# A new issue order for every engine of a clustered attention and feed-forward kernel

## The chip, the core and the metric

The kernel runs on one NeuronCore of a Trainium2 chip. The core has five engines with their own instruction queues, each of which runs in order: TensorE (PE; its weight loads are listed as PEld), VectorE (DVE), ScalarE (ACT), GpSimd (POOL) and SyncE (SP), which here only issues DMAs. The metric is the device time of one execution in microseconds, the median of several runs.

## The reference, cut to what matters

Attention of 4 batches x 8 heads x 768 tokens x 64 features, in which a query sees only the keys of its own cluster (the nearest of 16 centroids of its head), and then a feed-forward layer of 3072 tokens, 512 to 1024 to 512, with a softmax-weighted activation and a layer norm inside:

```python
q_assign = np.argmax(np.einsum('bhsd,hcd->bhsc', q_n, c_n), axis=-1)   # and k_assign
mask = q_assign[:, :, :, None] == k_assign[:, :, None, :]
scores = np.where(mask, scale * np.matmul(q, k.transpose(0, 1, 3, 2)), -1000000000.0)
attn = softmax(scores);  x = matmul(attn, v)        # heads side by side: 3072 x 512
h = x @ w_in
solu = h * softmax(h)
ln = (solu - mu) / np.sqrt(var + 1e-06) * g_ln
out = ln @ w_out
```

## The kernel before, in words

**Names.** The program is a list of about 1,800 small named operations. A name is a kind and an index; `ca1.0.1.1`, for example, is a cast for batch 1, head pair 0, k (1; q is 0), second head of the pair. The kinds, with their lines:

- SP: `ld` loads raw q or k of a head pair (L374 whole for batch 0, L402 in quarters of 96 KB after that), `lv` loads v (L518), `lo` and `li` load w_out and w_in (L555, L539), `tx` turns the attention output x into the feed-forward's left operand by a transposing DMA (L662), `tu` does the same for the activation u (L715), `ou` stores the output (L781).
- Attention operands: `tp` (PE, L386) with `xa` (copy out, L396), or `xt` (DVE, L410), turn raw q and k; `ca` casts them into the score operand `qk` (L434, L436, L438); `cv` casts v (L523). `cl` (PE, L448 and L453) scores the tokens against the centroids; `tb`, `mx`, `oh`, `ot` (DVE, L462, L475, L480, L486) turn that, take the maximum, make the one-hot rows and turn them back; `pl` places those rows below q and k in `qk` (L498 and L505 by an engine, L503 by a DMA), and `bl` blanks the rows of the other head (L514). The one-hot rows make the score of an own-cluster pair larger by a constant, which is how the mask gets into one matmul.
- Attention: `S` is one PSUM bank of scores (PE, L584), `E` its exponential (ACT, L590), `V` the product with v for 128 queries (PE, L607; a column of ones gives the denominator), `N` the division (DVE, L619 and L632) for a group of them.
- Feed-forward, 24 tiles of 128 tokens: `h` (PE, L693, four parts a tile), `hm` the row maximum (DVE, L699), `ex` the exponential (ACT, L705), `u` the product with h (DVE, L710), `bn` and `ag` the statistics (DVE, L721, L725), `at` and `al` the row's scale (POOL, L731, L737, L740), `y` (PE, L754, four parts a tile), `sc` the scaling (ACT L769 or DVE L771). The last tiles are turned on TensorE (`ptx`, `ptu`) and copied out by `tx` and `tu` operations of DVE or ACT (L674, L687, L689).
- Weights, once: `su` sums w_out times the gain (DVE, L559 and L562), `me` (PE) spreads the mean, `ce` centres w_out (DVE, L570), `wi` casts w_in (L542). `fl` are idle matmuls early on.

**Tiling.** Raw tiles have 8 buffers, turned ones 6, score operands 6 head pairs, score banks in PSUM 3, their exponentials 9. One PSUM bank collects `V` of a group until `N` has read it. Three banks take the halves of `h` of two tiles in turn.

**What sets the order.** `Weave.ORDER` holds, for every engine, a written-out list of kinds with counts (`ld4` is the next four `ld`), and `Weave.AWAY` says which operations run on another engine than the one they name by default. Within a kind and engine, operations come in the order in which they were added. `queues()` turns the lists into queues of names and asserts that every operation is used up; `run()` walks the queues with costs and due times, and issues the instructions in the order of the starts that it finds. Each engine's own order is therefore exactly its list. An instruction waits on its engine, with all that is behind it, until its operands and its buffer are there; the synchronisation is put in from the tiles that it reads and writes.

```python
for kind, n in re.findall(r"([A-Za-z]+)(\d*)", text):
    for _ in range(int(n or 1)):
        queues[e].append(of[e, kind].pop(0))
```

Of the kernel before, what the change touches and what calls it, by code (L numbers as in the profile page):

```python
# [22 lines left out]
class Weave:  # L23
# [19 lines left out]
    ORDER["PE"] = """
        wm tp2 cp tp cl tp fl5 cl tp2 S3 tp2 S2 cq S tp S tp S2 cl V3 S2 tp S gt tp S3 V3 cl S3 tp2
        S2 V2 S V S2 tp S2 tp S2 V3 S3 cl S V S2 V3 S3 cl S2 V S V2 S V S5 V2 S2 V2 S3 V S2 V2 S V
        S3 V3 S V S2 me S3 V3 S V S2 cl S2 V2 S2 V2 S h S h S2 h S h S2 V3 S V h S2 h V2 S V2 S2 h2
        S3 h2 S2 V4 S2 y3 V S y V S3 h2 S V2 S2 h2 V2 S cl S2 V2 h S2 h S h V S2 V3 S h S2 y3 S y V
        S2 V h y S3 y3 S h S2 V3 cl S2 V S V2 S y S2 y S V h S V y S h V S V y S3 V2 cl S2 h S V2 S2
        V S V2 S V S h S2 cl V4 S3 y2 S2 y S V S V2 S V S2 y S V2 S2 h2 S2 h V S2 V h S2 h V4 y2 S2
        y h y S2 V2 h S h S2 cl S V4 S2 h cl S3 h3 S2 V S V y S h S y V S y V3 S3 h y h S2 h V2 S2 y  # L50
        h2 S y S V2 S y V y V3 S3 h2 S2 cl h S2 h S cl S3 V4 y V y S3 y V y S3 h2 S V S V cl S V4 S2
        y S y S2 y V S y V S V S2 V y2 S y S2 V2 S V2 S2 y S V2 S2 V2 S h S2 h S h2 S2 V S h V y S y
        V3 h S y S2 y V S2 h2 V2 S V S V S cl S2 V h2 S y S V S2 h2 S3 y V S V2 h2 V2 S V S2 h2 S3
        h2 S V y S2 V2 y S V3 S h2 S h S2 V2 y V2 S y h y S3 h2 S2 V S y V3 S3 h2 y S V S h V2 h S3
# [19 lines left out]
    """
    AWAY = {}
    AWAY.update(dict.fromkeys("""
        ca0.0.0.0.1 ca0.1.1.0 ca0.2.0.0 ca0.2.1.1 ca1.3.0.0 ca2.2.0.0 ca2.3.1.0 sc23.0 tu22.1
        xa0.0.0.1 xa0.0.1.0 xa0.1.0.0 xa0.2.1.0 xa0.2.1.1
    """.split(), "ACT"))
    AWAY.update(dict.fromkeys("""  # L80
        bl1.2 ca0.1.0.1 ca1.3.0.1 ca2.1.0.1 ca3.2.0.1 ca3.3.0.0 cv0.1.0 cv1.0.1 cv1.1.1 cv2.0.0
        cv2.0.1 cv2.1.0 cv2.1.1 cv2.2.1 cv3.0.0 cv3.3.0 pl0.0.0.1.1 pl0.1.0.0 pl0.1.1.0 sc0 sc13
        sc14 sc19 sc20 sc22 sc23.1 sc9 tu22.0 wi3 xa0.0.0.0
    """.split(), "DVE"))
    AWAY.update(dict.fromkeys("""
        ca0.0.1.1.0 pl0.0.0.0.0 pl0.0.1.1.0 pl1.0.0.0 pl1.0.0.1 pl1.0.1.1 pl1.1.0.0 pl1.1.0.1
        pl1.1.1.0 pl1.1.1.1 pl1.2.0.0 pl1.2.0.1 pl1.2.1.0 pl1.2.1.1 pl1.3.0.0 pl1.3.0.1 pl1.3.1.0
        pl1.3.1.1 pl2.0.0.0 pl2.0.0.1 pl2.0.1.0 pl2.0.1.1 pl2.1.0.0 pl2.1.0.1 pl2.1.1.0 pl2.1.1.1
        pl2.2.0.0 pl2.2.0.1 pl2.2.1.1 pl2.3.0.0 pl2.3.0.1 pl2.3.1.1 pl3.0.0.0 pl3.0.0.1 pl3.1.0.1
        pl3.1.1.0 pl3.1.1.1 pl3.2.1.0 pl3.2.1.1 pl3.3.0.0  # L90
    """.split(), "POOL"))
    HOP = 0.17
    LANES = 8
# [1132 lines left out]
```

## Time and profile before

| | before |
|---|---|
| median of 3 runs | 228.74 us (228.43 to 230.03) |
| span of the profiled execution | 230.3 us |
| its own time beside the span | not given |
| PE busy | 218.3 us (95%) |
| DVE busy | 202.9 us (88%) |
| ACT busy | 195.9 us (85%) |
| POOL busy | 122.8 us (53%) |
| TensorE clock granted | 1.00 of full speed |
| moved by DMA | 39.15 MB, of which 115,128 of 125,472 packets are under 512 B |

The profile is of one execution; the span reaches from its first to its last instruction. Busy time is the union of an engine's instructions. Ends of matmuls are modelled, so a busy PE is not PE at its peak, and spans on POOL are rough. A group's row gives the line, engine, operation, tiles, shapes and count, then busy time, the mean of one in ns, and the idle time before them with what ended it. In the rows by stretch, each engine's busy time in the stretch comes in the order PE, PEld, DVE, ACT, POOL.

### The profile page before, as it was taken

The numbers are of one execution on the slowest core, as the hardware profiler recorded it, in microseconds if no ns is written. First come the engines' busy times: TensorE is split into PE (matmuls) and PEld (weight loads), VectorE is DVE, ScalarE is ACT, GpSimd is POOL, SyncE is SP. The second block draws the span as 40 slices with busy tenths as digits, with TensorE's granted clock in tenths as the row PEclk, the third lists the DMA queues.
The fourth block names the chain that finished last, engine by engine and source line by source line (L and its number), as shares of the span: only waits on it lengthen the run. The fifth ranks groups of instructions, "written<-read, shape, count | busy, mean of one in ns | idle before, by whom it ended". The sixth has DMA issues, their size and how long they took to land.

```text
span 230.3 us, 6600 instructions
## 1 busy us (share of the span) xinstructions
PE 218.3 (95%) x2393; PEld 149.0 (65%) x2424; DVE 202.9 (88%) x363; ACT 195.9 (85%) x379; POOL 122.8 (53%) x241
## 2 busy tenths in 40 slices
PE   6999898999999999899999899999999999999994
PEld 3566465767767777576667657786677777665352
DVE  3599999999999997999999879887998894987993
ACT  2689889999999999798999889999999998785350
POOL 4555789639663835593349969546915130233311
PEclk9999999999999999999999999999999999999999
DMA  6996989488799989999999999999245118668623
GB/s 147 358 311 151 245 174 324 161 162 150 151 195 175 158 221 170 131 250 160 201 149 204 183 163 197 222 170 238 56 100 128 47 25 124 152 94 178 177 78 117
DMA packets 125472, 39.15 MB, mean 170 GB/s; under 512 B 115128, under 2 KB 120192, under 8 KB 125440
## 3 DMA queue, kind: packets, MB, share of 16 engines
q1 hardware_dynamic: 123696, 38.21, 79.5%
q10 hardware_dynamic: 1744, 0.52, 0.9%
q8 instruction: 19, 0.31, 0.6%
q14 instruction: 13, 0.11, 0.2%
HBM read 23.11 MB, written 6.29 MB: 128 GB/s over the span
## 4 chain that ended last, share of the span: by engine, by line
PE 57%; DVE 19%; POOL 8%; DMA 6%; issue 4%; SPq 4%; ACT 1%; DVEq 0%; POOLq 0%; ACTq 0%
PE sps L584 16%; PE hreg L693 13%; PE yps L754 13%; PE ops L607 9%; PE csc L453 3%; DMA raw<-in_k_dram 3%; SPq L402 3%; DMA w_st<-in_moe_w_in_dram 3%; DVE xt L410 2%; DVE u L710 2%; POOL qk L505 2%; PE hreg L386 2%; POOL qk L436 2%; POOL qk L438 1%; DVE x L632 1%
## 5 line engine op out<-in xcount | busy, mean ns | idle before, releaser
L590 ACT ACTIVATE e<-sps 128x512 bf16<-128x512 f32 (+1 forms) x294 | 150.4, 605 | 11.0 <-PE sps L584 9.8
L584 PE MATMUL sps<-qk 96*128 96x256 bf16 (+5 forms) x636 | 95.5, 264 | 2.1 <-POOL qk L505 0.8
L584 PEld LDWEIGHTS <-qk 96*128 96x128 bf16 (+1 forms) x636 | 60.6, 121 | 30.6 <-issue 9.2
L607 PEld LDWEIGHTS <-e 128*128 128x128 bf16 x1152 | 50.2, 97 | 11.9 <-DVE x L632 1.6
L607 PE MATMUL ops<-v,e 128*128 128x65 bf16 x1152 | 54.7, 193 | 1.6 <-POOL v L523 0.9
L693 PE MATMUL hreg<-w_in_sb,xT 128*128 128x512 bf16 x176 | 49.1, 379 | 1.5 <-DVE u L710 0.6
L754 PE MATMUL yps<-w_out_c,uT 128*128 128x512 bf16 x169 | 46.9, 378 | 0.7
L705 ACT ACTIVATE e_sb<-hreg,nmax 128x1024 bf16<-128x1024 f32 x24 | 26.8, 1118 | 8.5 <-DVE nmax L699 8.3
L505 POOL COPY qk<-oht 32x384 f32<-32x384 f32 (+1 forms) x42 | 21.2, 504 | 22.8 <-DVE oht L486 16.1
L710 DVE TENSOR_TENSOR u<-e_sb,hreg 128x1024 bf16<-128x1024 bf16 x24 | 28.9, 1205 | 4.9 <-ACT e_sb L705 3.4
L721 DVE BATCH_NORM_STATS2 bs<-u 128x6 f32<-128x512 bf16 x48 | 31.5, 676 | 0.2
L699 DVE TENSOR_REDUCE nmax<-hreg 128x1 f32<-128x1024 f32 x24 | 28.9, 1206 | 2.3 <-PE hreg L693 2.2
L410 DVE STREAM_TRANSPOSE xt<-raw 128x768 f32<-128x768 f32 x24 | 23.1, 961 | 2.8 <-DMA raw<-in_k_dram 1.6
L754 PEld LDWEIGHTS <-uT 128*128 128x128 bf16 x200 | 17.9, 97 | 10.9 <-DVE uT L687 0.7
L438 POOL TENSOR_SCALAR qk<-xt 64x768 bf16<-64x768 f32 (+1 forms) x28 | 23.7, 848 | 1.6
L693 PEld LDWEIGHTS <-xT 128*128 128x128 bf16 x192 | 16.8, 97 | 11.0 <-DVE u L710 1.2
L737 POOL TENSOR_SCALAR esq<-es,mv 128x1 f32<-128x1 f32 x24 | 8.1, 339 | 27.8 <-DVE mv L725 22.7
L436 POOL CAST qk<-xt 64x768 bf16<-64x768 f32 (+1 forms) x25 | 20.4, 817 | 3.9 <-DVE xt L396 1.6
L731 POOL TENSOR_SCALAR es<-esum 128x1 f32<-128x1 f32 x24 | 5.9, 246 | 30.9 <-ACT e_sb L705 30.4
L632 DVE TENSOR_TENSOR x<-ops,den 128x256 bf16<-128x256 f32 (+1 forms) x39 | 18.9, 485 | 1.3
L740 POOL TENSOR_TENSOR alpha<-esq,halves 128x1 f32<-128x1 f32 x24 | 14.6, 606 | 2.0
L769 ACT ACTIVATE y<-yps,alpha 128x512 f32<-128x512 f32 x16 | 11.1, 694 | 2.7 <-PE yps L754 2.2
(77 smaller groups left out, 186.3 us busy)
## 6 DMA issues: line engine op xcount, KB each, us to landing
vf<-in_v_dram SPq DMA_DIRECT2D x16, 384.0 KB, 4.6
out_dram<-y SPq DMA_DIRECT2D x23, 256.0 KB, 3.3
raw<-in_q_dram SPq DMA_DIRECT2D x50, 96.0 KB, 3.3
raw<-in_k_dram SPq DMA_DIRECT2D x50, 96.0 KB, 3.3
w_g<-in_moe_w_out_dram SPq DMA_DIRECT2D x4, 512.0 KB, 6.8
w_st<-in_moe_w_in_dram SPq DMA_DIRECT2D x4, 512.0 KB, 6.5
raw<-in_q_dram SPq DMA_DIRECT2D x3, 384.0 KB, 6.6
raw<-in_k_dram SPq DMA_DIRECT2D x3, 384.0 KB, 7.1
```

Of the source, the lines that this page charges most:

```text
L410: nc.vector.transpose(xt[:], raws[b, p, i][:].rearrange("p j c -> p (j c)"))
L438: VEC[e].tensor_scalar(dst, src, scalar1=inv_C, scalar2=1.0, op0=Alu.mult, op1=Alu.mult)
L505: ins = VEC[e].tensor_copy(dst.bitcast(F32), src.bitcast(F32).unsqueeze(1) .to_broadcast([NB, 2, n // 2]))
L584: nc.tensor.matmul(sps_[n, k][:, c0:c0 + w], side(b, h // 2, 1, h % 2, keys)[r], side(b, h // 2, 0, h % 2, slice(s0 * P, s0 * P + w))[r])
L590: nc.scalar.activation(es[n, k][:, :w], sps_[n, k][:, :w], Act.Exp, scale=exp_scale, bias=-exp_scale)
L607: nc.tensor.matmul(opss[g][:, s, :VW], es[n, k][:, c0:c0 + P], v1[slot(b, h // 2)][:, h % 2, kt, :VW], start=(kt == 0), stop=(kt == n_t - 1))
L693: uses(nc.tensor.matmul(hreg[:, at(f, f2)[1], :], xTs[f][:, dc, :], w_in_sb[:, dc, f2 * FF2:(f2 + 1) * FF2], start=(dc == 0), stop=(dc == ...
L699: uses(nc.vector.tensor_reduce(ff[f, "nmax"][:], pair_of(f), axis=AXY, op=Alu.max, negate=True), *both(f))
L705: uses(nc.scalar.activation(ff[f, "e"][:], pair_of(f), Act.Exp, bias=ff[f, "nmax"][:], accum_out=ff[f, "esum"][:]), *both(f))
L710: uses(nc.vector.tensor_tensor(ff[f, "u"][:], ff[f, "e"][:], pair_of(f), op=Alu.mult), *both(f))
L721: nc.vector.bn_stats(ff[f, "bs"][:, f2, :], ff[f, "u"][:, f2, :])
L754: ins = nc.tensor.matmul(dst, ff[f, "uT"][:, at(f, f2)[0] * (n_fc // 2) + c, :], w_out_c[:, fc, cols], start=(fc == 0), stop=(fc == n_fc - 1))
```

## The change

All five lists of `ORDER` are rewritten, and `AWAY` is changed for 69 operations. The operations, their shapes and their buffers stay, and so do costs and due times. By engine, the lists differ in these counts (before, after):

| engine | kinds whose count changes |
|---|---|
| SP | `pl` 11, 19 |
| POOL | `ca` 53, 60; `cv` 22, 26; `wi` 3, 4; `pl` 52, 46; `bl` 16, 14 |
| DVE | `ca` 5, 2; `cv` 10, 6; `wi` 1, 0; `pl` 5, 3; `xa` 10, 9; `bl` 1, 3; `sc` 8, 10 |
| ACT | `ca` 10, 6; `sc` 17, 15; `xa` 6, 7 |
| PE | none |

In the two halves of the first pair, `ca` and `pl` are half as wide. The diff, cut (each list goes on):

```diff
     ORDER["SP"] = """
-        ld4 lv si ld4 lg lo ld4 lv ld3 lo ld3 lv ld2 lo ld lo ld3 lv ld2 li4 tx ld lv ld3 pl tx ld5
-        tu lv ld3 tx ld2 lv ld tu ld tu ou ld8 tu ld lv ou ld ou ld6 lv ld3 tu ld4 lv ou ld tx ld tu
-        ld4 lv ld tx ld ou ld3 tx tu ld3 lv ld ou ld tu ld6 pl lv ld2 pl ld6 tu ld4 ou2 tu2 ld3 lv2
...
+        ld4 lv si ld4 lo lg lv ld4 lv ld6 lo2 ld4 li2 ld4 lv2 lo ld2 li lv li ld2 tx2 pl ld3 lv ld2
+        tu ld6 tu ld pl ld4 lv ld3 ou tx ld2 tu ld3 ou ld tu ld2 lv ld6 lv pl ld ou ld3 tu ld7 tx pl
+        ld2 lv tu ld3 ou pl ou ld4 tx ld3 pl2 ld2 tu2 ld lv ld2 tx pl2 ou2 lv ld5 tu pl2 ou lv pl tu
...
     ORDER["POOL"] = """
-        po z ca4 cv pl2 bl pl2 bl ca z cv sg pl3 ca2 bl pl3 ca3 cv ca pl z bl cv2 pl4 ca2 bl cv2 wi3
-        z pl ca pl2 ca z ca2 at cv ca3 bl ca2 at pl2 al pl cv pl bl ca al pl4 at ca2 al ca2 cv2 at2
-        al pl3 bl pl2 cv2 ca3 at pl3 ca al ca2 bl al pl3 at2 pl bl ca al ca at ca pl2 ca pl al pl cv
...
+        ca3 pl bl pl3 ca2 pl cv2 ca3 pl4 z cv2 pl2 ca bl ca pl ca pl z2 ca sg pl2 ca bl pl2 ca wi
+        cv3 pl wi3 ca3 z pl2 po ca cv2 z ca bl ca2 cv at2 pl3 al ca bl at cv al pl ca2 cv pl bl pl2
+        cv al at ca3 cv at al ca3 pl3 bl ca5 cv pl al pl2 cv bl at al pl ca3 bl at cv2 ca3 pl2 at al
...
     ORDER["PE"] = """
...
-        V y2 S2 V h y S h S h S V h S V2 y3 S y S h2 V3 h2 S2 V y4 S2 h2 S V h2 S V y4 h2 V2 y4 h2
-        ptx y4 h2 y2 h2 ptu2 y8 ptu2 y6
+        V S h2 V y2 S2 h V y h V S2 y h2 S3 V3 y2 V y h2 S2 y h2 S y V4 S2 y3 S h4 S2 y3 S y h V4 h3
+        ptx y4 h2 y4 h2 ptu2 y10 ptu2 y6
     ORDER["DVE"] = """
...
-        u bn2 hm N u bn2 hm ag2 u N bn3 hm ag2 tx sc u bn2 hm tu sc ag u bn2 tu ag sc2
+        bn hm bn2 N u sc hm bn2 ag u N ag sc ag hm bn N u bn hm N bn u hm ag bn2 u N hm ag tx sc u
+        bn2 ag bn hm bn2 ag2 u bn2 ag tu2 sc
```

More of the change, by code (lines that the diff above doesn't have):

```diff
@@ L48 @@
[L48 to L52, printed above, removed]
@@ L76 @@
     AWAY.update(dict.fromkeys("""
[L77 to L78 removed]
+        ca0.0.0.1.1 ca0.2.0.0 ca0.2.1.1 sc23.0 tu22.1 xa0.0.1.0 xa0.1.0.0 xa0.1.0.1 xa0.2.0.0
+        xa0.2.1.1 xa0.3.0.0
     """.split(), "ACT"))
     AWAY.update(dict.fromkeys("""
[L81 to L83 removed]
+        bl0.0.1 bl0.1 bl2.3 ca0.0.0.0.0 ca3.2.1.0 cv0.0.0 cv0.2.1 cv2.1.0 cv3.2.0 cv3.2.1 cv3.3.0
+        pl0.0.0.1.1 sc0 sc1 sc13 sc14 sc18 sc23.1 sc4 sc7 sc8 sc9 tu23.0 xa0.0.0.0
     """.split(), "DVE"))
     AWAY.update(dict.fromkeys("""
[L86 to L90, printed above, removed]
+        ca0.0.1.0.0 pl0.0.1.0.0 pl0.0.1.1.0 pl1.0.0.0 pl1.0.0.1 pl1.0.1.0 pl1.1.0.1 pl1.1.1.0
+        pl1.1.1.1 pl1.2.0.0 pl1.2.0.1 pl1.2.1.0 pl1.2.1.1 pl1.3.0.0 pl1.3.0.1 pl1.3.1.1 pl2.0.0.1
+        pl2.0.1.0 pl2.0.1.1 pl2.1.1.1 pl2.2.0.0 pl2.2.1.0 pl2.3.1.1 pl3.0.0.0 pl3.0.0.1 pl3.0.1.0
+        pl3.1.0.1 pl3.1.1.0 pl3.1.1.1 pl3.2.1.1 pl3.3.0.1 pl3.3.1.0
     """.split(), "POOL"))
```

47 lines of the change are left out of this document (25 added, 22 removed).

## The prediction

> **What bounds the kernel now.** I read the page's busy rows and slices first, then its chain, then the busy times by stretch.
>
> ```profile
> span 230.3 us, 6600 instructions
> PE 218.3 (95%) x2393; PEld 149.0 (65%) x2424; DVE 202.9 (88%) x363; ACT 195.9 (85%) x379; POOL 122.8 (53%) x241
> DMA  6996989488799989999999999999245118668623
> PE 57%; DVE 19%; POOL 8%; DMA 6%; issue 4%; SPq 4%; ACT 1%; DVEq 0%; POOLq 0%; ACTq 0%
> ```
>
> TensorE is busy 95% of the span and carries 57% of the chain that ended last. The DMA engines are busy in nine tenths or more of most slices up to two thirds of the span. No edit changes what TensorE computes, so the gain can only come from its idle time, 230.3 - 218.3 = 12.0 us, and a loss from new idle time. The next view says where the idle time lies (the columns are the stretch, its length, then busy time of PE, PEld, DVE, ACT, POOL, the granted clock, the DMA share, GB/s).
>
> ```profile
> 20.00:30.00 10.00, 8.97 (x102) 5.85 (x98) 9.53 (x18) 8.28 (x19) 7.44 (x11) 1.00 0.99 232
> 30.00:40.00 10.00, 9.16 (x128) 6.20 (x126) 9.38 (x18) 9.84 (x21) 8.81 (x15) 1.00 0.93 242
> 34.00:44.00 10.00, 9.11 (x119) 6.10 (x116) 9.53 (x18) 9.98 (x21) 9.60 (x12) 1.00 0.83 271
> 60.00:80.00 20.00, 19.79 (x203) 13.74 (x204) 19.80 (x34) 19.01 (x36) 12.26 (x23) 1.00 1.03 171
> 80.00:96.00 16.00, 14.94 (x203) 11.01 (x203) 13.97 (x25) 14.72 (x30) 7.22 (x17) 1.00 0.95 179
> 96.00:112.00 16.00, 15.25 (x172) 11.25 (x174) 15.79 (x29) 14.87 (x29) 11.01 (x19) 1.00 1.02 195
> 112.00:132.00 20.00, 18.98 (x211) 13.05 (x213) 19.19 (x31) 18.78 (x36) 12.83 (x23) 1.00 1.05 180
> ```
>
> The reader is to see three things. From 20 to 40 us TensorE is idle 1.03 + 0.84 = 1.9 us while VectorE is at 95%. From 60 to 80 us there is nothing to win, 0.2 us. From 80 to 132 us TensorE is idle 1.06 + 0.75 + 1.02 = 2.8 us, with VectorE at 96 to 99% in the last two stretches. The granted clock is 1.00 throughout.
>
> **The change, part by part.** Term A, work that changes engine. I counted the named operations in the two lists and priced them by their groups (mean ns of one stands after the busy time).
>
> ```profile
> L436 DVE CAST qk<-xt 64x768 bf16<-64x768 f32 x5 | 4.5, 897 | 0.1
> L523 DVE CAST v<-vf 128x384 bf16<-128x384 f32 x10 | 4.6, 466 | 0.0
> L542 DVE CAST w_in_sb<-w_st 128x1024 bf16<-128x1024 f32 x1 | 0.7, 683 | 0.0
> L498 DVE COPY qk<-oht 32x384 f32<-32x384 f32 x2 | 1.6, 812 | 0.1
> L771 DVE TENSOR_SCALAR y<-yps,alpha 128x512 f32<-128x512 f32 x7 | 5.2, 738 | 0.6 <-POOL esq L737 0.4 <-POOL qk L505 0.2
> L436 POOL CAST qk<-xt 64x768 bf16<-64x768 f32 (+1 forms) x25 | 20.4, 817 | 3.9 <-DVE xt L396 1.6 <-ACT xt L396 1.0
> L523 POOL CAST v<-vf 128x384 bf16<-128x384 f32 x22 | 11.1, 521 | 1.0 <-DMA vf<-in_v_dram 0.5
> L505 POOL COPY qk<-oht 32x384 f32<-32x384 f32 (+1 forms) x42 | 21.2, 504 | 22.8 <-DVE oht L486 16.1
> ```
>
> VectorE loses the five whole casts of q (4.5 us), four v casts net (4 x 0.466 = 1.9), the w_in cast (0.7) and two places (1.6). It gains one half and one whole cast (about 1.3 at the same price) and two more scales (2 x 0.738 = 1.5); two more blanks and one copy of a turned half less cancel within the 0.5 us of a v cast. The sum is -8.7 + 2.8 = -5.9 us. GpSimd gains seven casts (7 x 0.817 = 5.7), four v casts (2.1) and the w_in cast (no more than twice VectorE's price, 1.4) and loses six places (3.0): about +6 us on an engine that is idle 47% of the span. ScalarE loses four casts and two scales. Eight places become DMAs issued by SyncE (11 before, 19 after). The work that left VectorE is worth something only where VectorE holds TensorE up. That is 96 to 132 us, 0.75 + 1.02 = 1.8 us of idle TensorE; the bounds are -1.8 and 0. I take two thirds, **-1.2 us**, because VectorE is at its fullest there and is ahead by several microseconds of queue by then.
>
> GpSimd's extra work has a price on VectorE, which the trace shows as spread (min, median, max in ns):
>
> ```profile
> L436 DVE CAST qk<-xt x5: 555/1044/1172, 14.0 to 164.0; 64x768 bf16<-64x768 f32 x5
> L480 DVE TENSOR_TENSOR oh<-cst,mx x17: 357/548/1133, 8.6 to 172.1; 128x384 bf16<-128x384 f32 x15, 128x192 bf16<-128x192 f32 x2
> ```
>
> The same cast took 0.555 us or 1.172 us, the same compare 0.548 or 1.133. If all 17 compares took the maximum, VectorE would lose 17 x 0.58 = 10 us; GpSimd's busy share rises by 6 of 230 us, so 10 x 6/230 is about **+0.2 us**, and below nothing is not excluded, since the exposed casts leave VectorE. [...]
>
> Term B, the first projection. The SyncE list moves two loads of v (lv1.0, lv1.1, 384 KB each) and two quarter loads (96 KB each) ahead of the last w_in load (li3), and two more quarter loads ahead of the first turn of x (tx0). Here is that spot before, from the timeline (start, duration), the waits, and the landing times of xT:
>
> ```profile
> 26.17 0.66 SPq L555 DMA_DIRECT2D w_g<-in_moe_w_out_dram  x1
> 34.42 1.99 SPq L539 DMA_DIRECT2D w_st<-in_moe_w_in_dram  x4
> 43.89 1.35 SPq L662 DMA_TRANSPOSE xT<-x  x1
> ...
> SPq L662 <- DVE xt L410: 8.3, 1, 8.3
> ...
> DMA to landing us min/median/max: 2.4/3.3/4.9
> ...
> 40.42 3.79 POOL L542 CAST w_in_sb<-w_st 128x1024 bf16<-128x1024 f32 x3
> 49.15 0.60 PE L693 MATMUL hreg<-w_in_sb,xT 128*128 128x512 bf16 x2
> 38.26 1.29 DVE L562 SCALAR_TENSOR_TENSOR w_sum<-w_g,g_ln,w_sum 128x512 f32<-128x512 f32 x1
> ...
> 119.17 0.35 PE L607 MATMUL ops<-v,e 128*128 128x65 bf16 x6
> ...
> 119.80 0.38 PE L584 MATMUL sps<-qk 80*128 80x256 bf16 x2
> ```
>
> Before, SyncE had issued all of w_in by 36.4 us, waited 8.3 us for x, and issued tx0 at 43.9 into a queue that had drained; the first h matmul ran at 49.15 us without an idle TensorE. After, the transfers ahead of li3 are 2 x 384 + 2 x 96 = 960 KB more. At 271 GB/s (34 to 44 us) that is 3.6 us, at 171 GB/s (60 to 80 us) 5.7 us; I take 4.3, nearer to the stretch where it happens. From it goes what the DMA engines left idle from 34 to 44 us, (1 - 0.83) x 10 = 1.7 us, of which I give back 1.5. The third w_in cast ended at 44.2 us, so li3 had landed at about 44; now at 44 + 4.3 - 1.5 = 46.8. Two more quarters, 0.9 us, and a turn's shortest landing, 2.4, put x in place at 50.1 us. TensorE comes to its first h earlier: it stands behind 67 score banks and 38 value groups in place of 70 and 40. Three banks and two groups are at most 3 x 0.38 + 2 x 0.35 = 1.8 us; matmuls in a row overlap, so I take 1.0, and TensorE is there at 48.1 us. It waits 2.0 us. The bounds are 0 (tx0 overtakes, or the loads cost no time) and 50.1 + 1.4 + 0.2 - 48.1 = 3.6 us with the slower rate. I take **+2.0 us**. [...]
>
> Two waits are added on the way. The fourth w_out load (lo3) now stands behind li0 and li1 and five quarters and two v loads more, 2,272 KB, 8.6 us at 271 GB/s. It was issued at 26.2 us and its sum ran at 38.3 us; behind that sum on VectorE stand N6 and so tx0, and I count 0 to 1 us, inside the bounds above. On GpSimd the last two w_in casts wait for li2 and li3, and behind them stand three casts and two places of pair (1,0), 3 x 0.817 + 2 x 0.504 = 3.5 us, done by about 46.8 + 1.3 + 3.5 = 51.6; the scores that want them come about 5 us after the first h (53.7 before). They cost nothing.
>
> Term C, the head-of-line wait at 90 to 96 us:
>
> ```profile
> 90.95 0.98 DVE L410 STREAM_TRANSPOSE xt<-raw 128x768 f32<-128x768 f32 x1 [1.58 <-DMA raw<-in_k_dram]
> ...
> 95.44 0.99 PE L607 MATMUL ops<-v,e 128*128 128x65 bf16 x24 [0.90 <-POOL v L523]
> ```
>
> VectorE waited 1.58 us for a raw k tile, which made the one-hot turn of pair (2,0) (ot2.0) late; GpSimd's place pl2.0.1.0 waited for it, and the cast of v of pair (1,3) stood behind that place, and TensorE waited 0.90 us for the cast. After, cv1.3.0 and cv1.3.1 stand far ahead of any place of pair (2,0). The wait goes; next late is the bank's normalise, on VectorE. Bounds -1.06 (the stretch's whole idle time) and 0; I take **-1.0 us**.
>
> Term D, the tail:
>
> ```profile
> 222.28 1.23 DVE u L710
> 223.54 1.29 DVE bs L721 x2
> 225.21 1.93 PE hreg L754 x16
> 227.24 0.48 DVE e_sb L771
> ```
>
> After the last u, VectorE now does two bn, one aggregate and both copies of the turned u, where ScalarE took one copy; a copy of one half and the aggregate are below half the 1.29 us of the two bn, so +0.6. The last two bn and two aggregates now also stand ahead of that u, up to +0.4. Against it, TensorE's last h stands two y parts earlier in its list, 4 matmuls of full width; 16 of half width took 1.93 us, so -1.0. I take **0**, bounds -1.0 and +1.0.
>
> The sum is -1.2 + 0.2 + 2.0 - 1.0 + 0 = 0.0 us, for a span of 230.3 us. The page has no time of its profiled execution beside the span; the median of the runs shown, 228.74 us, is 1.6 below that span, and I carry this difference over unchanged: about **228.7 us**. The measurement of this kernel can tell about 1% (2.3 us) from no change, so my forecast is "within 1%".
>
> **The rivals.** *Covered start* (faster). The DMA idle time at 44 to 60 us and the earlier queue let tx0 land before TensorE comes, term B is 0, and the freed VectorE also gives back half of the 1.9 us of 20 to 40 us: -1.2 + 0.2 + 0 - 1.0 - 0.9, and the rest of the 1.8 us, -0.6, is -3.5: 225.2 us. For it: VectorE is the full engine there. Against it: all that is gained before 48 us is waited for again if tx0 is late.
>
> *Transposes behind loads* (slower). By the first y of tile 6 the list has 88 loads of raw q and k in place of 76 ahead of its turn tu6, and 7 places in place of 1, with one turn of x fewer.
>
> ```profile
> 113.45 1.28 SPq L715 DMA_TRANSPOSE uT<-u  x1
> 119.37 0.59 PE L754 MATMUL yps<-w_out_c,uT 128*128 128x512 bf16 x2
> ...
> DMA to landing us min/median/max: 3.0/3.9/5.4
> ```
>
> Twelve quarters and six places are 12 x 96 + 6 x 48 = 1,440 KB, 8.2 us at 180 GB/s; less one turn (1.3) and less what the DMA engines left idle from 34 to 44 us (1.7) and from 80 to 96 us (0.8), 4.4 us remain. The turn was issued 5.9 us ahead of its y and takes 3.9 to land, so 2.0 us is its slack. It decides from the point where the loads cost more than that slack. TensorE would then wait 2.4 us there, and since it waits, term A's 1.2 us buys nothing: 0.0 + 2.4 + 1.2 = 3.6, 232.3 us. For it: the DMA engines are at 1.0 of their time from 60 to 132 us. Against it: a load can't be issued before its buffer is free, and TensorE's own delay of term B adds to the slack.
>
> *GpSimd late* (slower). GpSimd runs in order with 6 us more work; if its places and casts arrive late at three pairs by the 0.9 us of term C, it is 0.0 + 2.7: 231.4 us. Against it: 47% idle.
>
> That the change does not do what it says can hardly be: each list must use up every operation.
>
> **How the numbers follow.** Forecast 0.40, covered start 0.27, transposes behind loads 0.22, GpSimd late 0.11. Faster by over 1% is 0.27, within 1% 0.40, slower 0.33. The likeliest alone reaches from 226.5 to 231.0. The range takes in the rivals and the far bounds of terms B and D: from 225.0 (covered start) to 233.0 (232.3 with part of the 1.0 of the tail).
>
> **What would show it.** Step B: an idle TensorE ahead of the first h, x landing near 50 us, no 8.3 us wait of SyncE. Step A: VectorE's busy time near 197 us and less idle TensorE from 96 to 132 us. Step C: no wait of TensorE for a v cast near 95 us. The slower rival: waits of h or y matmuls for a turn between 100 and 150 us. I am wrong if the head from 10 to 48 us itself moves by more than a microsecond, which I have priced at nothing.

## The result, and the profile after

The changed kernel takes 246.42 us (median, 245.37 to 248.12), the kernel before, run beside it, 229.12 us. The ratio is 1.0757, 95% interval 1.0699 to 1.0815: 17.3 us slower. I had forecast 228.7, with a range up to 233.0. The ratios leave out executions that are more than 1.5% above the fastest of the same kernel, the medians do not.

The page of the changed kernel: the span, the first busy row, the granted clock by slice, the chain by engine.

```profile
span 243.5 us, 6592 instructions
...
PE 220.3 (90%) x2392; PEld 149.4 (61%) x2424; DVE 200.4 (82%) x356; ACT 196.9 (81%) x374; POOL 126.0 (52%) x245
...
PEclk9997999999999999999799999999999999999999
...
PE 60%; DMA 12%; DVE 10%; ACT 6%; issue 4%; SPq 3%; POOL 3%; DVEq 0%; ACTq 0%; POOLq 0%
```

The profiled execution took 245.37 us, 1.9 more than its span. TensorE is idle 243.5 - 220.3 = 23.2 us (before 12.0), and the transfers have doubled their share of the chain. The clock row has two slices at 0.7, where before all stood at full clock. The busy times by stretch (columns as before):

```profile
20.00:30.00 10.00, 9.25 (x100) 5.80 (x100) 6.36 (x12) 6.54 (x14) 5.21 (x11) 0.83 0.98 237
30.00:40.00 10.00, 8.43 (x106) 4.87 (x103) 8.40 (x17) 8.51 (x15) 6.01 (x12) 1.00 0.94 227
...
96.00:112.00 16.00, 14.60 (x176) 10.90 (x179) 14.19 (x26) 13.83 (x28) 9.46 (x17) 1.00 1.06 187
112.00:132.00 20.00, 16.79 (x168) 10.89 (x169) 13.46 (x22) 14.22 (x27) 8.46 (x15) 0.91 0.87 156
```

From 20 to 40 us VectorE is no longer full (6.36 and 8.40 of 10 us), and TensorE still loses time. From 112 to 132 us TensorE is idle 3.2 us in place of 1.0. What TensorE waited for (in us: in total, times, longest), first in the whole run, then from 0 to 50 us:

```profile
PE sps L581 <- ACT e L587: 5.2, 11, 1.7
PE hreg L690 <- DMA xT<-x: 3.3, 4, 1.4
PE yps L751 <- DMA uT<-u: 3.0, 1, 3.0
...
PE sps L581 <- DVE qk L511: 1.1, 1, 1.1
```

```profile
PE sps L581 <- ACT e L587: 4.9, 10, 1.7
```

None of these four was among the waits before. The scores waited for exponentials, nearly all of it in the first 50 us. The last view is the first and last start (after the durations) of the feed-forward matmuls, of before and of the changed kernel:

```profile
L693 PE MATMUL hreg<-w_in_sb,xT x176: 377/378/390, 49.1 to 219.2; 128*128 128x512 bf16 x176
L754 PE MATMUL hreg<-w_out_c,uT x16: 272/273/283, 225.2 to 226.9; 128*128 128x256 bf16 x16
```

```profile
L690 PE MATMUL hreg<-w_in_sb,xT x171: 377/378/390, 54.3 to 231.8; 128*128 128x512 bf16 x171
L751 PE MATMUL hreg<-w_out_c,uT x16: 272/273/283, 238.3 to 240.0; 128*128 128x256 bf16 x16
```

The loss in these two traces has two parts: about 5 us by the first projection (49.1, then 54.3), and 8 us between it and the last `y` (177.8, then 185.7). From the last `y` to the end it is 3.4 and 3.5 us. Together that is the difference of the spans, 243.5 - 230.3 = 13.2 us, and not 17.3: the profiled execution of before was a long one. Its span alone is above the median time of 229.12, while the other executions on record took about 2 us more than their spans. So the step of my prediction from the span to the time, 1.6 us down, started from an unusual execution.

### The profile page after: what moved, and what is told of

It is laid out like the page before. It is cut to its first block, busy times and chain, and to the rows that moved or that the text cites. A ratio compares the mean times of both kernels' runs of the same rounds, so it can differ in the third digit from the quotient of the medians.

```text
span 243.5 us, 6592 instructions
## 1 busy us (share of the span) xinstructions
PE 220.3 (90%) x2392; PEld 149.4 (61%) x2424; DVE 200.4 (82%) x356; ACT 196.9 (81%) x374; POOL 126.0 (52%) x245
## 4 chain that ended last, share of the span: by engine, by line
PE 60%; DMA 12%; DVE 10%; ACT 6%; issue 4%; SPq 3%; POOL 3%; DVEq 0%; ACTq 0%; POOLq 0%
PE sps L581 19%; PE hreg L690 13%; PE yps L751 10%; PE ops L604 10%; DMA xT<-x 6%; ACT e L587 5%; DMA raw<-in_q_dram 3%; PE csc L450 3%; DMA uT<-u 3%; DVE bs L718 2%; DVE u L707 2%; PE csc L445 2%; DVE nmax L696 1%; PE hreg L383 1%; POOL qk L495 1%
## 5 line engine op out<-in xcount | busy, mean ns | idle before, releaser
L587 ACT ACTIVATE e<-sps 128x512 bf16<-128x512 f32 (+1 forms) x294 | 154.5, 596 | 25.5 <-PE sps L581 22.4
L581 PE MATMUL sps<-qk 96*128 96x256 bf16 (+5 forms) x636 | 97.7, 266 | 8.5 <-ACT e L587 5.2
L581 PEld LDWEIGHTS <-qk 96*128 96x128 bf16 (+1 forms) x636 | 59.8, 121 | 33.2 <-issue 16.0
L690 PE MATMUL hreg<-w_in_sb,xT 128*128 128x512 bf16 x171 | 47.2, 379 | 4.5 <-DMA xT<-x 3.3
L433 POOL CAST qk<-xt 64x768 bf16<-64x768 f32 (+1 forms) x31 | 25.3, 817 | 7.0 <-DVE xt L393 3.5
L502 POOL COPY qk<-oht 32x384 f32<-32x384 f32 (+1 forms) x34 | 16.3, 480 | 20.9 <-DVE oht L483 18.0
L407 DVE STREAM_TRANSPOSE xt<-raw 128x768 f32<-128x768 f32 x24 | 22.3, 953 | 2.2 <-DMA raw<-in_k_dram 2.2
L734 POOL TENSOR_SCALAR esq<-es,mv 128x1 f32<-128x1 f32 x24 | 9.0, 375 | 24.5 <-DVE mv L722 21.5
L520 POOL CAST v<-vf 128x384 bf16<-128x384 f32 x26 | 13.3, 531 | 5.5 <-PE sps L581 2.9
L766 ACT ACTIVATE y<-yps,alpha 128x512 f32<-128x512 f32 x14 | 9.6, 688 | 6.3 <-PE yps L751 4.8
```

Source lines behind the costliest of these rows:

```text
L407: nc.vector.transpose(xt[:], raws[b, p, i][:].rearrange("p j c -> p (j c)"))
L433: VEC[e].tensor_copy(dst, src)
L581: nc.tensor.matmul(sps_[n, k][:, c0:c0 + w], side(b, h // 2, 1, h % 2, keys)[r], side(b, h // 2, 0, h % 2, slice(s0 * P, s0 * P + w))[r])
L587: nc.scalar.activation(es[n, k][:, :w], sps_[n, k][:, :w], Act.Exp, scale=exp_scale, bias=-exp_scale)
L690: uses(nc.tensor.matmul(hreg[:, at(f, f2)[1], :], xTs[f][:, dc, :], w_in_sb[:, dc, f2 * FF2:(f2 + 1) * FF2], start=(dc == 0), stop=(dc == ...
```

## The experiments

A ratio is to the kernel before on the same chip; its difference is turned into us with 229.12. The changed kernel stands at 1.0757. It was timed once, beside a kernel before of 229.12 us; beside the experiments the kernel before took 230.28 to 231.12 us. By the plain difference of medians, a gain on the changed kernel would be 1 to 2 us smaller than the one given here.

### The start

**Theory "ring".** All idle matmuls (`fl`) write one tile, `idle_p`, that has the tag of the score banks, of which there are three (L215). Before, all five ran ahead of the first scores. The changed list spreads them, the last ahead of piece 15 at 49.3 us, and the bank is theirs until then. Two banks are left, and a score bank waits for the exponential two banks back.

fl_early, on the changed kernel:

```diff
-        wm tp2 cp tp cl tp fl cl tp2 S3
...
-        S2 fl S tp S tp S2 V2 S V S2 tp S fl2 S2
...
+        wm tp2 cp tp cl tp fl5 cl tp2 S3
...
+        S3 tp S tp S2 V2 S V S2 tp S3
```

> The changed kernel with one edit: the five short idle matmuls run in a row before the second centroid similarity, as in the kernel before; TensorE's list is otherwise that of the changed kernel. Theory 'ring': the idle matmuls write into one of the three PSUM banks of the scores, and the changed kernel keeps that bank from the scores until the last of them has run at 49.3 us; with it free from 10 us on, TensorE no longer waits for the exponentials two pieces back (4.9 us in 0 to 50 us), 'PE sps L581 <- ACT e' falls below 1 us, the first projection comes back towards 48 us, and the time is 240.5 us (239 to 242). Rival 'operand copies': ScalarE's exponentials are late for ScalarE's own reasons (copies moved ahead of them), the waits stay, and the time is 245 to 247.5 us.

Measured 243.58 us, ratio 1.0552 (1.0481 to 1.0624): 4.7 us faster than the changed kernel. Its waits, and the operation that held VectorE next:

```profile
PE ops L604 <- DVE x L629: 2.2, 1, 2.2
...
PE sps L581 <- ACT e L587: 0.7, 3, 0.3
```

```profile
37.33 0.98 DVE L407 STREAM_TRANSPOSE xt<-raw 128x768 f32<-128x768 f32 x1 [2.36 <-DMA raw<-in_k_dram]
```

The wait for exponentials went from 5.2 to 0.7 us, as "ring" says. TensorE was then early enough to meet the next late thing: a raw k tile that VectorE waited 2.36 us for, with the division that TensorE needs behind it. So the first projection came only to 52.1 us, and TensorE's waits for turns of x grew from 3.3 to 6.4 us.

fl_late, on the kernel before, gives the reverse:

```diff
-        wm tp2 cp tp cl tp fl5 cl tp2 S3
...
+        wm tp2 cp tp cl tp fl cl tp2 S3
...
+        V3 S3 cl S2 fl S
+        tp2 S2 V2 S V S2 tp S2 fl2 tp S2
...
+        V S3 V3 S V fl S2 me
```

> The kernel before with one edit: its five short idle matmuls are spread as in the changed kernel (one behind the first transposes, one and two among the scores of pieces 2 and 4, the last ahead of piece 15). Theory 'ring': waits of the scores for the exponentials appear up to the last idle matmul, and the time is 233 to 235 us. Rival 'operand copies', or any cause that lies in the changed order of the other engines: 229.1 us within 1.

Measured 241.92 us, ratio 1.0433 (1.0322 to 1.0544), with the same wait:

```profile
PE sps L584 <- ACT e L590: 5.9, 14, 1.5
```

Five small matmuls, moved and nothing else, cost the kernel before 9.9 us, more than the 4 to 6 that I expected. One of its four executions had a mean clock of 1.00 and took 238.7 us, 8.0 more than the kernel before beside it (230.69). The others, at 0.970 to 0.972, took 241.8 to 244.4; by this difference I estimate that the clock (below) added 3 to 6 us to them.

head_undone and head_alone swap the whole start, up to the first projection, on all engines:

```diff
# head_undone, on the changed kernel, PE; SP, POOL, DVE and ACT likewise
-        wm tp2 cp tp cl tp fl cl tp2 S3 cq tp S tp S tp S tp S tp S2 cl S V3 S tp S gt S tp S2 V3 cl
+        wm tp2 cp tp cl tp fl5 cl tp2 S3 tp2 S2 cq S tp S tp S2 cl V3 S2 tp S gt tp S3 V3 cl S3 tp2
...
```

> The changed kernel with the start of the kernel before: on every engine, all that the kernel before ran ahead of its first projection (49 us) is in the old order and on the old engines; what comes later is as changed. Theory 'head': the first projection is at 49 to 50 us in place of 53.95 and the end comes 5 us earlier, near 241.5 us (240 to 243); the rest of the loss lies behind 50 us. Rival 'all of the loss is the head, the rest follows from it': 229 to 233 us. Rival 'the head is made up for later': 245 to 247 us.

> The kernel before with the start of the changed kernel, up to its first projection (53.95 us); what comes later is in the old order and on the old engines. Theory 'head': 4 to 6 us slower than the kernel before (and up to 9 where a second half-clock stretch falls into the start). Rival 'the head is made up for later': within 1 us of the kernel before.

Measured 241.66 us, ratio 1.0466 (1.0401 to 1.0531), and 238.28 us, ratio 1.0311 (1.0238 to 1.0385). The start is worth 6.7 us when undone and 7.1 alone; what lies behind it costs 10.7 us (head_undone over before). The 7.1 of the one kernel and the 10.7 of the other make 17.8, the 17.3 of the whole change within the intervals, so the parts add. The first and last starts of head_undone:

```profile
L690 PE MATMUL hreg<-w_in_sb,xT x192: 377/379/391, 49.1 to 228.0; 128*128 128x512 bf16 x192
L751 PE MATMUL hreg<-w_out_c,uT x16: 272/273/283, 234.5 to 236.2; 128*128 128x256 bf16 x16
```

The first projection is back at 49.1 us, and from it to the last `y` it is 187.1 us, 1.4 more than in the changed kernel (185.7): what is lost behind the start is still lost.

### The clock

In the changed kernel the granted clock was halved twice before its end, each time behind a stretch in which TensorE stood idle about half the time or more. By stretch, ahead of and in its two half-clock times:

```profile
17.99:21.41 3.42, 1.71 (x29) 0.99 (x30) 2.31 (x6) 2.73 (x6) 3.14 (x6) 1.00 0.94 132
21.41:24.82 3.41, 3.37 (x19) 1.41 (x12) 1.37 (x3) 1.21 (x3) 1.02 (x3) 0.50 1.03 261
113.57:116.98 3.41, 1.08 (x6) 0.64 (x7) 2.96 (x5) 1.40 (x3) 1.79 (x3) 1.00 1.01 217
116.98:120.39 3.41, 3.41 (x25) 2.07 (x24) 0.70 (x2) 1.63 (x3) 2.52 (x6) 0.50 0.95 194
```

TensorE was busy 1.71 and 1.08 us of 3.41, and the 3.41 us after that ran at 0.50, which is 1.7 us of work lost each time: four `y` matmuls in a row took 1.91 us there (at 117.85 us), four at full clock 1.04 (at 115.90). The four executions had mean clocks of 0.986, 0.977, 0.979 and 0.986. The mean, 0.982, gives 0.018 x 245 = 4.4 us of the 17.3 as an estimate, and an upper one: it counts every lost cycle as lost time. fl_late's executions at 0.970 to 0.972 lost 6.7 to 7.2 us by this sum and took 3 to 6 more than the one at 1.00; head_undone's at 0.984 and 0.993 took 241.34 and 241.71. y5_fill fills the second wait with work:

```diff
                 ff[f, "y"] = ps_m.tile([P, d_model], F32, name="yps", tag="m")[:]
+                if f == 5:
+                    for _ in range(12):
+                        nc.tensor.matmul(ff[f, "y"], ident_b[:], w_out_c[:, 0, :])
```

> The changed kernel with twelve matmuls of 512 columns (about 2.5 us) put ahead of y of tile 5, into the PSUM bank that y of tile 5 then starts afresh; they depend on nothing late. TensorE's wait of 3.0 us for the transposed u at 112.9 us is so filled with work, but no shorter. Theory 'the clock follows the idle time': the half-clock stretch of 3.41 us behind that wait goes, the granted clock of the run rises by 0.007, and the time falls by 1.7 us against the changed kernel (1 to 2.5). Rival 'the clock dips for another reason (the load of the matmuls that follow, or time)': the dip stays, the time is that of the changed kernel or up to 0.5 us more.

Measured 245.4 us, ratio 1.0632 (1.0547 to 1.0718). The filler ran at 114.67 us, and the stretch at which the clock had fallen, and the one behind it, read:

```profile
114.67 2.76 PE L748 MATMUL yps<-w_out_c,ident_b 128*128 128x512 bf16 x12
```

```profile
115.50:118.90 3.40, 3.05 (x16) 1.37 (x15) 2.95 (x5) 1.39 (x3) 1.60 (x2) 1.00 1.01 218
118.90:122.30 3.40, 3.40 (x44) 2.44 (x42) 0.71 (x2) 2.75 (x5) 2.14 (x5) 1.00 0.94 191
```

That half-clock stretch is gone. Without the filler TensorE would have been busy about 1.1 us of the first of these stretches (3.05 less the 1.93 of the filler that lie in it), as in the changed kernel; with it the clock stayed. So in this execution idle time was the cause, and useless work prevented the fall. The time fell by 2.9 us by the ratios, but the two intervals overlap, so a gain is not shown. The mean clock of the profile did not rise: 0.986 over 243.2 us is two half-clock times of 3.41 us, as in the changed kernel, so one more fell elsewhere. Over the four executions it was 0.987 in place of 0.982.

### The transposes and SyncE's order

The turn of u of tile 5 was issued at 109.2 us behind a permutation copy, parts of a token load and a load of v; it landed 6.7 us later, and `y` waited:

```profile
106.69 0.62 SPq L500 DMA_DIRECT2D qk<-oht  x1
107.37 1.15 SPq L399 DMA_DIRECT2D raw<-in_q_dram  x2
108.62 0.47 SPq L515 DMA_DIRECT2D vf<-in_v_dram  x1
109.19 1.26 SPq L712 DMA_TRANSPOSE uT<-u  x1
...
DMA to landing us min/median/max: 3.0/3.2/6.7
...
115.90 1.04 PE L751 MATMUL yps<-w_out_c,uT 128*128 128x512 bf16 x4 [2.99 <-DMA uT<-u]
```

This is my slower rival's mechanism, at another tile. Three kernels issue transposes earlier.

```diff
# tu5_first, on the changed kernel, SP
-        ld3 tu ld7 tx pl ld2 lv tu ld3 ou
+        ld3 tu ld7 tx tu pl ld2 lv ld3 ou
# tr_early, on the changed kernel: 21 of the tx and tu as early as their data was there
# tr_five, on head_undone
-        pl ld4 lv ld3 ou tx ld2
+        pl ld4 lv ld3 tx ou ld2
-        ld3 tu ld7 tx pl ld2 lv tu ld3 ou
+        ld3 tu ld6 tx ld pl ld tu ld lv ld3 ou
-        tx ld2 lv tu2 ld4 ou pl ou tx2 ou
+        tx tu ld2 lv tu ld4 tx ou pl ou tx ou
```

> The changed kernel with one edit on SyncE: the transpose of u of tile 5 is issued ahead of one permutation load, two parts of a token load and one load of v, instead of behind them. Theory 'transposes behind loads': the transpose lands some 4 us earlier, the 3.0 us wait of y of tile 5 goes, and with it the half-clock stretch that follows it: 241.7 to 243.5 us. Rival: the wait only moves to the next late transpose or to the loads that now come later, and the time is 245.5 to 247.5 us.

> The changed kernel with one edit on SyncE: every transpose of x and u stands as early in its list as its data was there in the changed kernel's trace (21 of them move, by 1 to 20 places; that of tile 4 of x was ready at 62.95 us and issued at 78.28). All else in the old order. Theory 'transposes too late in the list': the waits for xT and uT (6.3 us in all) fall below 2 us and the half-clock stretch at 117 us goes: 6 to 8 us faster than the changed kernel, about 239 us. Rival 'what is issued later in their place (token and permutation loads) is late instead': the waits move to the scores, and the time is within 1.5 us of the changed kernel.

> The changed kernel with the start of the kernel before, and five transposes issued a little earlier on SyncE: that of x of tile 4 ahead of the store of tile 0, of x of tile 6 ahead of one part of a token load, of u of tile 5 ahead of one part of a token load and the load of v, of u of tile 10 ahead of three loads, of x of tile 14 ahead of two stores and a permutation load. They pass 1, 1, 2, 3 and 3 places, not up to 20 as in the run before. Theory 'a transpose behind a large load or a waiting store is late, and the clock doubles the price': against the run with the old start alone, the waits for xT and uT (6.8 us) fall below 2 and the half-clock stretch at 112 us goes: 5 to 7 us faster, 235 to 237 us. Rival 'the wait moves to what is passed': within 1.5 us of 241.7.

Measured: tu5_first 248.21 us, ratio 1.0796 (1.0723 to 1.0869), no gain. tr_early 245.21 us, ratio 1.0653 (1.0558 to 1.0747), 2.4 us by the ratios, with overlapping intervals, where I expected 6 to 8. tr_five 242.76 us, ratio 1.0474 (1.0401 to 1.0548), no gain on head_undone's 1.0466. All three miss what I expected. The rivals' times held in tu5_first (247.4 us by its ratio) and in tr_five; tr_early lies between the two theories. The wait that was removed came back elsewhere: in tu5_first, among others, at the scores, for a copy of the permutation, in tr_early at ScalarE's scaling of `y`, which waited for a store that was passed and held the exponentials behind it, in tr_five at `y`, for the bank that another such scaling frees. A row of each:

```profile
PE sps L581 <- DMA qk<-oht: 1.6, 1, 1.6
```

```profile
118.12 0.69 ACT L766 ACTIVATE y<-yps,alpha 128x512 f32<-128x512 f32 x1 [3.27 <-DMA out_dram<-y]
```

```profile
171.82 1.46 PE L751 MATMUL yps<-w_out_c,uT 128*128 128x512 bf16 x4 [2.15 <-ACT y L766]
```

So a late transpose was what TensorE met first, and taking it away gained little or nothing. sp_alone, the kernel before with the changed SyncE list (and its one engine-forced difference, its own 11 copies):

```diff
-        ld4 lv si ld4 lg lo ld4 lv ld3 lo
...
+        ld4 lv si ld4 lo lg lv ld4 lv ld6
...
```

> The kernel before with the changed order of SyncE alone (the DMA issues), every other list as before. Theory 'transposes behind loads': transposes come late for h and y here too, 232 to 236 us. Rival 'the order of DMA issues costs nothing by itself, only together with the later lists of the other engines': 229.1 us within 1.

Measured 269.83 us, ratio 1.17 (1.1632 to 1.1768). The kind is as expected (16.5 us of waits for uT, 9.9 for xT), the size far over it. The order of one queue fits only the lists that it was written with, so this run says nothing on what that queue costs in the changed kernel.

### The work that changes engine

moves_body makes the 39 engine changes between 60 and 213 us on the kernel before, moves_pl only the 16 of them that are copies of the permutation (`pl`), moves_rest only the other 23. Each operation stands where it ran before.

```diff
# moves_pl, AWAY: 12 copies go from GpSimd to SyncE's DMA, 4 the other way
-        pl1.1.0.0 pl1.3.1.0 pl2.0.0.0 pl2.1.1.0 pl2.1.0.0 pl2.1.0.1 pl2.2.1.1 pl2.2.0.1
-        pl2.3.0.0 pl2.3.0.1 pl3.2.1.0 pl3.3.0.0
+        pl2.2.1.0 pl3.0.1.0 pl3.3.1.0 pl3.3.0.1
```

> The kernel before with the changed engines alone, for the 39 operations that move between 60 and 213 us (casts of v, operand copies, copies of the permutation, scales of y); each stands in its new engine's list at the time at which it ran in the trace of before, all else in the old order. Term A of the prediction: 1.0 us faster than before (1.2 gained less 0.2), ratio 0.995. Rival 'the moves cost by themselves (a permutation load that becomes a DMA issue on SyncE takes longer than GpSimd's copy, a cast on GpSimd waits in its list)': 1 to 4 us slower.

> The kernel before with the engine moves of 16 copies of the permutation alone (12 from GpSimd to a DMA that SyncE issues, 4 the other way), each put where it ran in the trace of before. Theory 'permutation on SyncE': the 4.2 us that all 39 moves of the body cost lie here, 3 to 5 us slower than before. Rival 'casts and scales': within 1 us of before.

> The kernel before with the other 23 engine moves of the body alone (casts of v, operand copies, two zeroings, four scales of y). Theory 'permutation on SyncE': 1 us faster to 1 us slower than before, since these moves take work off VectorE and ScalarE. Rival 'casts and scales': 3 to 5 us slower, with TensorE's similarities waiting for scales of y (2.1 us in the run with all moves).

Measured: moves_body 235.34 us, ratio 1.0194 (1.0152 to 1.0235); moves_pl 235.91 us, ratio 1.0216 (1.015 to 1.0282); moves_rest 231.53 us, ratio 1.003 (0.9999 to 1.006). The copies carry all of the cost, about 4.9 us; the casts, zeroings and scales give nothing. In moves_rest the idle TensorE from 96 to 132 us (1.8 us before) is gone, and similarities wait 2.1 us for scales of `y` instead:

```profile
96.00:132.00 36.00, 36.00 (x413) 25.46 (x414) 34.42 (x57) 32.93 (x65) 26.89 (x48) 1.00 0.91 185
...
PE csc L451 <- ACT y L767: 1.4, 1, 1.4
PE csc L451 <- DVE y L769: 0.7, 1, 0.7
```

In moves_pl one copy is met late, and the clock falls behind it (mean clock 0.992):

```profile
PE sps L583 <- DMA qk<-oht: 2.9, 1, 2.9
```

one_pl moves that copy alone:

```diff
# SP, on the kernel before
-        ld6 lv ld3 tu ld4 lv ou ld tx ld tu
+        ld6 lv ld3 tu ld4 lv ou ld tx ld pl
+        tu
# POOL
-        al pl3 bl pl2 cv2 ca3 at pl3 ca
+        al pl3 bl pl2 cv2 ca3 at pl2 ca
```

> The kernel before with one operation moved: the copy pl2.0.0.0 of a permutation (0.50 us on GpSimd at 99.6 us, first of the four inputs of the scores at 101.9 us) becomes a DMA that SyncE issues behind the transpose of x of tile 6. Theory 'one late copy and the clock behind it': the scores wait 2.9 us for its landing, a half-clock stretch of 3.41 us follows, 3.5 to 5 us slower than before, ratio 1.015 to 1.022. Rival 'the 12 copies cost a little each': within 1 us of before.

Measured 231.44 us, ratio 1.0062 (1.0032 to 1.0092): 1.4 us, between the two theories. The copy is issued at 98.71 us, lands 3.0 us later, and the scores wait:

```profile
98.71 0.66 SPq L503 DMA_DIRECT2D qk<-oht  x1
...
DMA to landing us min/median/max: 3.0/3.0/3.0
...
PE sps L584 <- DMA qk<-oht: 1.9, 1, 1.9
```

GpSimd's copy took 0.50 us (the group in the prediction). The profiled execution had the half-clock stretch, the others not: its mean clock was 0.993, theirs 0.998 to 1.000. So this one copy cost 1.4 us, and the execution with the half-clock stretch was the longest of the eight (232.78 us, the others 230.66 to 232.14); that moves_pl's 4.9 is several copies and the clock is what is left, not shown one by one.

The copies were then put back on their old engines in the changed kernel: pl_back0 with the old start, pl_back with the old start, the five transposes of tr_five and the edit of tr_five_dve below, fl_pl with the start as changed but the idle matmuls early.

```diff
# pl_back0, pl_back and fl_pl, AWAY
-        pl2.2.1.0 pl3.0.1.0 pl3.3.1.0 pl3.3.0.1
+        pl1.1.0.0 pl1.3.1.0 pl2.0.0.0 pl2.1.1.0 pl2.1.0.0 pl2.1.0.1 pl2.2.1.1 pl2.2.0.1
+        pl2.3.0.0 pl2.3.0.1 pl3.2.1.0 pl3.3.0.0
```

> The changed kernel with the start of the kernel before, and the 16 copies of the permutation back on their old engines, each placed behind the time at which its input was ready. Theory 'permutation on SyncE': SyncE no longer stands behind a wait for the one-hot (4.9 us in the run without this edit), the transposes come earlier, 2.5 to 5 us faster than that run (241.66): 237 to 239 us. Rival 'the later order itself': 240.5 to 243 us.

> The changed kernel with two edits only: the five idle matmuls in a row before the second centroid similarity, and the 16 copies of the permutation on their old engines. If the two costs are separate causes in the changed kernel itself, they add: 4.7 us and 5.5 us off the changed kernel, ratio to the kernel before 1.03 (1.02 to 1.035), near 237 us. Rival 'the later waits take the place of those removed, as they did for the transposes': ratio 1.045 to 1.06.

> As the run before in this list, and with the five earlier transposes and the two earlier operations on VectorE of the run that gave 239.82 us. Theory 'permutation on SyncE': the scores' wait of 1.7 us for a permutation load goes, and no transpose stands behind one: 235 to 237.5 us. Rival 'the later order itself': 239 to 241 us.

Measured: pl_back0 235.8 us, ratio 1.0228 (1.0156 to 1.03), 5.5 us off head_undone, more than expected, and not in the way that I expected: SyncE's longest wait for the one-hot (4.9 us in head_undone) stayed, at 5.7. TensorE's waits for turns of u fell from 3.4 to 1.0 us and its wait for a zeroing from 2.0 to 0.6, and the half-clock stretch went. fl_pl ratio 1.0348 (1.0281 to 1.0415): the two small edits take 9.4 us off the changed kernel, of 10.2 if they only added. This ratio rests on two executions of four; the median of all, 240.05 us over 230.28, is a ratio of 1.0424 and 7.6 us. pl_back 239.97 us (237.6 to 244.6, before 231.12), where I expected 235 to 237.5. It has pl_back0's copies, and the five transposes and two operations on VectorE moved earlier: these made it 4.2 us slower by the medians, and its trace has a wait of 3.2 us for another turn at 118 us and a half-clock stretch at 120.9. What TensorE still waits for in pl_back0, whose profile has no half-clock stretch before its end:

```profile
PE hreg L691 <- DMA xT<-x: 3.8, 4, 1.2
...
PE yps L752 <- DMA uT<-u: 1.0, 1, 1.0
```

### VectorE's order, and term C

```diff
# tr_five_dve, on tr_five, DVE
-        xt bn xt bl ot u sc mx
+        xt bn bl sc xt ot u mx
# cv_first, on the kernel before, POOL
-        al pl3 bl pl2 cv2 ca3
+        al pl3 bl pl cv2 pl ca3
```

> The kernel of the run before in this list, and on VectorE two operations (the zeroing bl2.3 that the change moved there, and the scale of y of tile 8 that it moved there) ahead of the transpose of the raw k that waits for its load at 146 to 149 us, instead of behind it. Theory 'head-of-line on VectorE': the scores' wait of 2.0 us for bl2.3 and the wait of 0.7 us for the scale go: 2 to 3.5 us faster than the run before. Rival 'the late load of k itself is next': no more than 0.5 us.

> The kernel before with one edit: GpSimd casts both halves of v of block 3 of head pair 1 ahead of the copy of a permutation (pl2.0.1.0) that it stood behind. Term C of the prediction: TensorE's wait of 0.9 us for that cast at 95 us goes, 1.0 us faster than before, ratio 0.995 to 0.997. Rival 'absorbed by the next wait': within 0.3 us of before.

tr_five_dve took 239.82 us, ratio 1.0386 (1.0336 to 1.0436), 2.0 us under tr_five with intervals that overlap a little. It takes two operations that the change gave to VectorE from behind this one, which waits for its load (rows of the changed kernel):

```profile
152.98 0.98 DVE L407 STREAM_TRANSPOSE xt<-raw 128x768 f32<-128x768 f32 x1 [2.24 <-DMA raw<-in_k_dram]
154.09 0.38 DVE L511 MEMSET qk<- 16x384 f32 x1
```

cv_first took 230.94 us, ratio 0.9991 (0.9962 to 1.0021): no difference. The wait for the cast is gone from its trace, and the next one, 1.1 us for a turn of x, takes its place:

```profile
PE hreg L693 <- DMA xT<-x: 1.1, 1, 1.1
```

No version was faster than the kernel before.

## Why the prediction was wrong

**The start, "priced at nothing", failed first.** I had written that I was wrong if the head from 10 to 48 us moved by more than a microsecond. It costs 6.7 to 7.1 us, and the bank that the idle matmuls hold costs the changed kernel 4.7 (fl_early). I had read of the `fl` only that they are idle and early. The tag of the tile that they write, and where the last of them stands, would have shown a pool of three banks cut to two until 49 us.

**Term A had the wrong sign.** I counted that eight places (net) become DMAs on SyncE and gave them no price; all 39 moves cost 4.4 us in place of a gain of 1.0, and the copies alone as much. The trace before had both prices: 0.50 us for the copy on GpSimd, and for the 11 that were DMAs already, from issue to landing,

```profile
DMA to landing us min/median/max: 1.9/2.5/3.7
```

In moves_pl and one_pl such a landing stood on the path to the scores (waits of 2.9 and 1.9 us). In the changed kernel's own trace TensorE waits for none; there the copies cost 5.5 us as a group (pl_back0), and by which path stays open. VectorE's busy time fell to 200.4 us, not to the 197 that I had named as a sign. The 0.2 us that I added for GpSimd's work beside VectorE is too small for any run here to show. The spread that it came from is there in both traces: of 30 compares of 384 columns, the seven that took 0.62 to 1.18 us ran beside a cast on GpSimd, the twelve with nothing on GpSimd beside them took 0.52 to 0.56. The rest of the term was right on its place and not on its worth: in moves_rest the idle time at 96 to 132 us goes, all 1.8 of it, and waits for scales of `y` at 82 and 143 us take it back.

**Term B did not bind.** TensorE came to its first projection, at 54.3 us, without an idle wait. li3 was issued at 40.2 us, the first turn of x only at 50.2, after a wait of 7.0 us for VectorE (I had said that no such wait would stay):

```profile
40.16 1.81 SPq L536 DMA_DIRECT2D w_st<-in_moe_w_in_dram  x1
...
50.17 4.87 SPq L659 DMA_TRANSPOSE xT<-x  x2
...
SPq L659 <- DVE cst L459: 7.0, 1, 7.0
...
49.51 0.18 DVE L616 RECIPROCAL den<-ops 128x4 f32<-128x4 f32 x1 [0.65 <-PE ops L604]
```

The last row is the division of x just ahead of the turn, which itself waited for TensorE. The turn was late because scores and divisions were late, not because it stood behind loads. No run shows whether a turn can pass loads that were issued before it; that it can't was an assumption of mine under the 2.0 us.

**Term C** was right on the wait and wrong on its worth: -0.2 us (-0.9 to +0.5) in place of -1.0. **Term D** held: from the last u to the end it is 8.0 us (from 222.28) and 8.7 (from 234.84), inside its bounds.

**The rival "Transposes behind loads"** named a wait that appeared, at tile 5 in place of 6, 3.0 us in place of 2.4. But undoing it bought no gain clear of the noise, three times. *Covered start* could not come, with the start itself late. *GpSimd late* did not show: TensorE waited 0.3 us for GpSimd in all, before 2.0.

**What no term held is the clock**: up to 4.4 us of the 17.3, paid behind waits that I would have priced at their own length. It lies inside the parts below, not beside them.

In all, by the ratios, 17.3 us is 6.7 for the start, 5.5 for the copies of the permutation, and 5.2 left. These lie behind the first projection; two operations behind a waiting one on VectorE may be 2.0 of them. The rest stays open: pl_back0 still waits 4.8 us for transposes, which before it hardly did, but no kernel that issued them earlier was faster by more than the noise.

## What to carry to other kernels

Look up which buffer every moved instruction writes, useless ones too: a tile that is written once more, late, takes its bank from a rotating pool until then (4.7 us in fl_early). In one_pl the price of a copy that went from an engine to a DMA on the path was in its landing (3.0 us, of which the scores waited 1.9), not in its issue (0.66). In tu5_first, tr_early and tr_five, removing the wait that one saw moved it to the next; swapping whole stretches or groups of moves on both kernels told more than mending single waits.

## What I had not expected of the hardware

In these traces the granted clock fell to half for 3.41 us, or a multiple (10.24 us in fl_late, from 44.74), after a stretch of 3.41 us in which TensorE was busy about half the time or less. In the 20 profiles (before, after and 18 experiments), 27 such stretches at full clock had TensorE busy below 55%, and the next was at half clock after 23 of them; of 1,270 stretches that were busier, after 4, and never where TensorE was busy 75% or more. The stretches lie on one grid in each profile: the two falls of the changed kernel, at 21.41 and 116.98 us, are 28.0 of them apart, those of fl_late, at 20.84 and 44.74, 7.0. Rows of two more kernels, one_pl and fl_late:

```profile
99.69:103.10 3.41, 1.45 (x14) 0.97 (x12) 3.35 (x7) 1.40 (x4) 2.25 (x4) 1.00 0.98 170
103.10:106.51 3.41, 3.41 (x24) 2.31 (x23) 0.46 (x1) 1.99 (x5) 0.00 (x0) 0.50 0.57 86
```

```profile
17.43:20.84 3.41, 1.82 (x12) 1.05 (x11) 2.40 (x5) 3.24 (x8) 1.55 (x3) 1.00 0.85 141
20.84:24.26 3.42, 3.38 (x35) 1.73 (x34) 1.76 (x4) 0.86 (x2) 1.55 (x3) 0.50 1.12 230
```

The longest single idle times ahead of these falls were shorter than 3.41 us: 2.99 us (after, at 116.98), 1.9 us (one_pl) and 1.5 us (fl_late, at 20.84). Executions of one kernel differ: one of fl_late's four had a mean clock of 1.00, the others 0.970 to 0.972; the profiled one of one_pl had 0.993, the other seven 0.998 to 1.000. Why they differ, no run here tests.
